# Another written order for SyncE's transfers and GpSimd's operations in a polysketch attention kernel with token mixing

## Chip, cores and metric

The kernel runs on one core of a Trainium2 chip. The metric is the device time of one execution in microseconds (us); the median of several runs is given. Engines are named as in the profile: PE (TensorE), DVE (VectorE), ACT (ScalarE), POOL (GpSimd) and SP (SyncE); SP and POOL are the two that issue DMA transfers here.

## The reference

Four batches, four heads, 1088 positions, head dimension 32, sketch size 8, so that all heads together are 128 wide. Inputs are float32, the weights arrive as float64.

```python
def phi(x):                                   # S1, S2: 8 x 32
    a = einsum('rd,bhsd->bhsr', S1, x)
    b = einsum('rd,bhsd->bhsr', S2, x)
    return einsum('bhsi,bhsj->bhsij', a, b).reshape(..., 64)
q_p, k_p = phi(q), phi(k)
kv = einsum('bhsf,bhsd->bhfd', k_p, v)
z = sum(k_p, axis=2)
x = einsum('bhsf,bhfd->bhsd', q_p, kv) / (einsum('bhsf,bhf->bhs', q_p, z) + 1e-6)
x = x.transpose(0, 2, 1, 3).reshape(4, 1088, 128)

theta = x @ w_theta
y = einsum('ts,bsd->btd', w_tok_r, x * cos(theta)) + einsum('ts,bsd->btd', w_tok_i, x * sin(theta))
u = x + y
out = u + maximum(u @ w_ch, 0)
```

The two token mixings, 1088 × 1088 × 128 for each of four batches and twice, are most of the arithmetic. They are computed with fewer products than that, in the manner of Strassen.

## The kernel before

**Tiles.** The 1088 positions are padded to nine chunks of 128. q, k and v of a batch are one tile of 128 partitions × 1152 columns each, in buffers of the class `big` (22 of 1152 columns). The token weights are 17 rows of blocks, each 1088 wide in two halves of 544; two half rows are loaded together as 64-bit words into a `zs` buffer (L614, 1088 KB) and rebuilt to float32: ACT makes a high part (L619) and a step (L621), DVE shifts the high part, and the step is added either by DVE or by an accumulating DMA that POOL issues (`join`, L348).

**The order is written out.** The program first records every operation (about 1150) with its engine, buffers and dependences; a call of `op` names the engine by a letter, "P" for PE, "V" for DVE, "A" for ACT, "G" for POOL, "S" for SP. Then `run` takes them in the order of the list `SEQUENCE`, whose numbers are the operations' indices, and gives each buffer the slot that the list `PLACES` says; `issue` emits them in that order. Each engine executes its own operations in the order of the list and waits for what they depend on, the former users of a slot included. No scheduler works after that.

**Stages, in order.** (1) `small`, `scaled`: the sketch matrices are unpacked, scaled and cut into parts. `rests` (L481) makes the sums `sf` and `sq`, `blocks_k` (L523) the head table `sbk` for the keys, `blocks_t` (L527) the table `sbt`, `sliced` (L491) the parts `cm`, `c16` and `cf`, `blocks_m` (L537) the head tables `mv` and `mf` of batch 0 for the queries, and `blocks_again` (L551) copies these to batches 1 to 3. `spread2` and `spread3` (L568, L589) serve a small product (L576) and its table `pbd`. All of these run on POOL.
(2) `key_sums` (L667): each batch's keys are rounded to a coarse level `kb` (bfloat16); PE sums kb·kb and the rest's products, from which a bound on the denominators is taken. For batches 1 to 3 the rest's product needs k + kb, which is made by loading k a second time into a buffer `kh` (L699, on SP) and adding kb to it with a `join` on POOL (stage names `keys1` to `keys3`; batch b's `rest` products on PE wait for it).
(3) `kfeatures`, `chain`, `query_slices`, `levels`: key features and their sums with v, and the queries' levels. `levels` (L1018) multiplies the queries by `mv` and `mf`; it is the first reader of the head tables.
(4) `numerators`, `theta_stage`, then the products of the mixing. Names in the prediction: `m70`, `m60`, `m30` are products of batches 0 and 1 (`product`, L1286) with sums of weight blocks; `ac30`, `ac20`, `ac40` (`asum`, L1275) are the accumulates that make these sums, eight `join`s each, one for each row block; `ac10` is such a sum on DVE. a11, a12, a21 and a22 are the quarters of the weights. `carry` adds a kept partial product to x by a `join`. `aj..` are the sums of smaller blocks later (L1525).

**Names of transfers.** `rowp3L` is the load and the rebuilding of the left halves of weight rows in pair 3, `rowp3R` the right halves, `row16` the last row. The lists below give POOL's and SP's share of the order.

```python
    def join(n, dst, src, w, r):                                                  # L346
        op("G", n * 2.55e-3, lambda: G.dma_start(dst(), src(), accum_op=ALU.add), w, r, kind=2)
    ...
        if KDMA[b]:                                                               # L697, batches 1 to 3
            op("S", n * 512 / 410e3, lambda: SY.dma_start(flat(kh()), k[b]...), [kh], [], kind=1)
    ...
        if KDMA[b]:                                                               # L707
            join(n, lambda: flat(kh()), lambda: flat(kb()), [kh], [kb])
    ...
    def run(self, sequence, places, fills):
        self.order = [self.ops[i] for i in sequence]
        for b, i in zip(self.bufs, places):
            b.slot = i
```

Of the kernel before, what the change touches and what calls it, by code (L numbers as in the profile page):

```python
# [52 lines left out]
    57, 58, 36, 233, 79, 10, 15, 54, 34, 59, 60, 61, 62, 95, 63, 51, 65, 66, 35, 38, 236, 131, 134, 16, 238,  # L53
    295, 136, 17, 67, 27, 182, 185, 68, 18, 69, 22, 137, 187, 241, 37, 183, 322, 242, 96, 237, 70, 239, 71, 72,
    73, 21, 210, 211, 212, 169, 306, 159, 74, 75, 80, 291, 293, 220, 296, 186, 28, 170, 29, 175, 221, 101, 243,
    81, 82, 83, 184, 346, 89, 176, 177, 297, 308, 30, 234, 244, 323, 240, 235, 84, 85, 86, 178, 222, 188, 213,
    90, 309, 307, 43, 87, 310, 326, 223, 102, 245, 163, 88, 311, 164, 91, 312, 214, 103, 19, 23, 246, 247, 248,
    92, 189, 215, 324, 386, 112, 104, 325, 93, 97, 44, 132, 105, 313, 347, 98, 463, 113, 39, 389, 455, 328, 464,
    249, 465, 466, 459, 460, 461, 462, 456, 457, 458, 171, 190, 191, 192, 193, 160, 99, 388, 194, 195, 196, 197,
    198, 133, 467, 33, 165, 20, 329, 261, 94, 166, 300, 108, 468, 114, 387, 172, 161, 469, 226, 135, 327, 139,  # L60
    470, 25, 350, 410, 348, 349, 471, 351, 100, 106, 199, 200, 162, 352, 298, 115, 107, 110, 472, 250, 201, 202,
    203, 204, 205, 353, 227, 206, 251, 252, 253, 262, 473, 207, 138, 394, 392, 109, 413, 299, 411, 474, 263,
    301, 140, 402, 475, 302, 208, 412, 254, 111, 255, 256, 257, 476, 258, 259, 264, 141, 142, 303, 46, 209, 260,
    45, 143, 144, 216, 145, 146, 477, 478, 147, 148, 149, 150, 151, 152, 267, 395, 397, 153, 268, 154, 390, 304,
    330, 155, 47, 24, 479, 403, 156, 157, 480, 481, 338, 484, 487, 485, 405, 491, 158, 269, 404, 265, 494, 492,
    173, 270, 266, 495, 482, 26, 271, 40, 305, 124, 483, 500, 493, 486, 48, 499, 332, 496, 391, 125, 488, 489,
    501, 272, 273, 497, 167, 490, 179, 118, 331, 274, 314, 502, 275, 116, 276, 126, 119, 277, 41, 120, 168, 174,
    503, 504, 505, 315, 450, 42, 341, 224, 180, 692, 632, 339, 127, 128, 217, 688, 689, 690, 506, 121, 340, 279,
    396, 684, 691, 218, 400, 693, 694, 122, 695, 685, 686, 687, 696, 283, 697, 498, 318, 278, 319, 117, 123,
    228, 698, 333, 699, 316, 515, 517, 282, 370, 700, 398, 229, 701, 702, 507, 509, 317, 181, 510, 452, 373,  # L70
    129, 511, 703, 230, 704, 219, 518, 354, 401, 508, 512, 130, 434, 516, 225, 526, 513, 231, 399, 524, 232,
    705, 286, 706, 709, 720, 710, 519, 451, 707, 708, 713, 525, 284, 520, 336, 521, 561, 514, 562, 563, 564,
    337, 371, 453, 557, 558, 553, 554, 555, 556, 408, 559, 716, 560, 334, 393, 436, 714, 723, 721, 362, 724,
    454, 634, 285, 715, 522, 717, 372, 335, 528, 565, 722, 711, 712, 342, 435, 566, 718, 344, 343, 356, 567,
    719, 355, 365, 725, 527, 726, 418, 409, 523, 568, 406, 569, 345, 570, 571, 730, 530, 732, 280, 281, 357,
    407, 635, 572, 531, 426, 529, 532, 533, 662, 727, 288, 748, 573, 574, 589, 542, 582, 750, 590, 591, 733,
    592, 593, 320, 585, 586, 583, 584, 419, 637, 594, 595, 587, 588, 575, 576, 321, 751, 578, 734, 608, 579,
    440, 736, 813, 577, 610, 821, 822, 823, 752, 374, 728, 739, 824, 747, 580, 364, 741, 375, 289, 376, 537,
    639, 377, 754, 742, 617, 729, 814, 437, 358, 441, 815, 416, 438, 611, 735, 749, 359, 816, 753, 817, 731,
    539, 612, 818, 439, 417, 819, 534, 743, 738, 740, 737, 755, 756, 414, 764, 758, 422, 745, 744, 619, 746,  # L80
    761, 763, 360, 361, 363, 757, 614, 415, 759, 420, 424, 378, 581, 820, 599, 368, 825, 826, 827, 613, 596,
    421, 762, 601, 620, 638, 621, 760, 536, 597, 598, 425, 607, 765, 609, 766, 772, 636, 369, 602, 603, 769,
    828, 366, 367, 538, 615, 600, 423, 605, 427, 627, 630, 829, 830, 831, 633, 616, 604, 606, 643, 428, 771,
    381, 379, 382, 774, 541, 430, 380, 626, 384, 629, 623, 645, 642, 429, 618, 432, 385, 640, 622, 383, 535,
    832, 442, 883, 768, 433, 624, 628, 540, 287, 833, 631, 834, 835, 836, 444, 448, 443, 446, 839, 840, 770,
    647, 641, 650, 658, 773, 644, 543, 655, 788, 837, 838, 544, 431, 767, 775, 777, 661, 646, 445, 653, 786,
    625, 841, 842, 844, 843, 845, 846, 667, 651, 670, 447, 776, 859, 449, 861, 927, 934, 648, 847, 660, 793,
    850, 778, 656, 649, 668, 791, 545, 652, 672, 789, 852, 657, 862, 863, 864, 669, 790, 1007, 865, 848, 867,
    659, 792, 665, 853, 679, 858, 654, 666, 928, 549, 779, 550, 860, 671, 866, 810, 849, 851, 546, 854, 855,
    794, 681, 683, 796, 663, 802, 801, 1009, 664, 856, 857, 877, 787, 868, 1025, 674, 798, 809, 800, 880, 1028,  # L90
    1026, 676, 870, 1010, 680, 682, 878, 871, 884, 881, 907, 1008, 890, 900, 872, 873, 806, 888, 547, 936, 892,
    909, 1014, 926, 678, 797, 869, 1032, 874, 902, 886, 1006, 891, 876, 932, 889, 875, 879, 548, 882, 911, 1027,
    804, 805, 893, 782, 1011, 887, 799, 894, 783, 551, 552, 807, 795, 1016, 1017, 895, 784, 803, 785, 906, 780,
    1029, 1046, 1012, 1018, 1019, 673, 1013, 1024, 1023, 898, 808, 1047, 1035, 1015, 904, 885, 899, 897, 896,
    912, 1044, 905, 677, 919, 910, 913, 916, 675, 903, 1031, 1022, 1020, 951, 811, 1030, 1045, 901, 940, 943,
    917, 933, 925, 915, 1021, 914, 918, 922, 1048, 1058, 1050, 812, 1053, 1049, 920, 924, 1060, 1033, 1037,
    1052, 923, 1051, 930, 945, 908, 929, 1034, 969, 1040, 931, 1041, 1054, 1056, 935, 1059, 1038, 937, 939,
    1057, 1062, 1055, 1061, 1070, 1071, 938, 946, 944, 947, 968, 1042, 1043, 1066, 1091, 1092, 1093, 962, 1039,
    781, 941, 942, 1065, 1064, 960, 1063, 1067, 1094, 950, 963, 1095, 1105, 952, 1096, 1097, 1098, 1068, 1069,
    1036, 1072, 1099, 1083, 961, 964, 1075, 1100, 1073, 1101, 1074, 1079, 1084, 1085, 949, 1076, 1080, 1081,  # L100
    948, 1102, 966, 1111, 958, 1077, 1078, 956, 965, 1086, 1082, 971, 957, 974, 973, 921, 967, 970, 972, 1087,
    975, 1088, 953, 982, 977, 983, 1110, 1089, 1090, 1002, 1003, 978, 979, 954, 959, 980, 976, 1004, 1005, 1106,
    981, 1123, 1112, 994, 995, 1116, 1104, 996, 987, 1109, 997, 1107, 990, 991, 1103, 992, 993, 1108, 984, 988,
    1130, 1133, 1134, 1115, 985, 955, 1125, 1135, 986, 989, 1114, 1117, 1121, 1126, 998, 1124, 999, 1000, 1136,
    1128, 1001, 1113, 1120, 1119, 1118, 1131, 1129, 1122, 1127, 1132, 1137, 1138, 1139, 1140, 1142, 1143, 1144,
    1145, 1141, 1146,
)
PLACES = (
    55, 59, 47, 48, 58, 2, 0, 2, 6, 7, 4, 11, 8, 21, 12, 7, 9, 24, 2, 46, 28, 3, 62, 61, 41, 45, 1, 60, 54, 47,
    56, 45, 46, 59, 48, 61, 51, 47, 54, 45, 61, 61, 41, 55, 49, 34, 60, 39, 58, 46, 36, 57, 44, 57, 52, 35, 54,  # L110
    47, 61, 49, 61, 56, 41, 60, 48, 36, 56, 42, 56, 50, 35, 55, 41, 61, 47, 34, 52, 50, 30, 9, 7, 60, 59, 43,
    53, 14, 59, 60, 16, 58, 43, 55, 38, 60, 40, 56, 34, 60, 43, 60, 37, 46, 51, 31, 10, 15, 59, 57, 39, 52, 13,
    57, 56, 60, 42, 58, 37, 56, 42, 60, 38, 55, 44, 62, 34, 29, 49, 29, 5, 12, 56, 62, 40, 45, 8, 55, 51, 47,
    52, 46, 53, 54, 59, 50, 45, 59, 46, 55, 51, 52, 53, 54, 49, 59, 50, 45, 61, 54, 53, 61, 40, 56, 58, 57, 32,
    56, 58, 56, 28, 55, 58, 56, 33, 57, 55, 58, 31, 17, 20, 18, 10, 3, 11, 1, 2, 13, 21, 14, 16, 8, 9, 6, 15,
    12, 22, 19, 23, 13, 26, 6, 23, 4, 22, 6, 24, 21, 26, 7, 24, 19, 25, 0, 22, 4, 25, 15, 26, 19, 26, 7, 22, 7,
# [1586 lines left out]
```

## Time and profile before

| what | value |
|---|---|
| runs | 222.5, 223.35, 222.51 us; median 222.51 |
| the profiled execution | 222.03 us |
| its span, first to last instruction | 220.3 us |
| PE clock granted | 1.00 |

How to read it. The span is the profiled execution from its first to its last instruction. A group or a waits row names line, engine and operation, and its tiles as out<-in; `[0.45 <-POOL sbk L334]` means that the engine stood idle 0.45 us before the instruction and that POOL's work on `sbk` ended that wait. In a timeline the first number is the start in us from the span's start, the second the duration. A `DMA_DIRECT2D` on POOL or SP is the issuing of a transfer; "DMA to landing" is the time from issue until the data is there. A table of stretches gives, for each, the busy time of PE, its weight loads, DVE, ACT and POOL with the count of instructions, the clock, the DMA engines' share and what they moved.

### The profile page before, as it was taken

Reading aid. Unit: us, or ns where it says so; the run is one execution under the profiler, and the core shown is the slowest. Engines: PE = TensorE matmul, PEld = TensorE weight load, DVE = VectorE, ACT = ScalarE, POOL = GpSimd, SP = SyncE. Lnnn points to the kernel's source line nnn. Section 1 sums busy time; section 2 is a strip of 40 time slices with the busy share of each in tenths; the row PEclk is TensorE's granted clock in tenths of the full one; section 3 lists DMA queues with packets and bytes.
Section 4 is the critical chain, followed back from the end, with each engine's and each line's share of the span. In section 5 each row is a group of like instructions: output and inputs, shape, how many; then the busy total and the mean of one; then the engine's idle time right before and its main releaser. Section 6 shows DMA issues by size and latency. Waiting matters only on the chain.

```text
span 220.3 us, 4200 instructions
## 1 busy us (share of the span) xinstructions
PE 212.1 (96%) x1481; PEld 177.1 (80%) x1481; DVE 188.1 (85%) x449; ACT 131.1 (60%) x277; POOL 80.7 (37%) x119
## 2 busy tenths in 40 slices
PE   7998999989999999999999999999999999999992
PEld 4697999976898796778888887888887888887882
DVE  2798999989999999999999999989999669567352
ACT  3896999979989899999989632662510100000000
POOL 1057934211013042064360746934360459251000
PEclk9999999999999999999999999999999999999999
DMA  6999999999759979987999999999998639688332
GB/s 207 407 415 409 349 354 389 358 419 376 233 171 285 296 239 226 316 210 124 190 261 176 276 192 189 189 183 189 185 134 124 96 46 149 93 122 112 61 56 53
DMA packets 34969, 48.78 MB, mean 221 GB/s; under 512 B 19204, under 2 KB 22276, under 8 KB 34820
## 3 DMA queue, kind: packets, MB, share of 16 engines
q0 software_dynamic: 10368, 18.21, 47.3%
q1 hardware_dynamic: 24580, 30.30, 40.8%
q8 instruction: 12, 0.20, 0.3%
q14 instruction: 9, 0.07, 0.1%
HBM read 28.07 MB, written 2.23 MB: 138 GB/s over the span
## 4 chain that ended last, share of the span: by engine, by line
PE 69%; DVE 18%; DMA 7%; issue 2%; ACT 2%; SPq 1%; ACTq 0%; DVEq 0%
PE ps L354 64%; DMA big<-hf 4%; DVE big L334 4%; DMA big<-k_l 3%; DVE g L334 3%; DVE big L338 2%; PE ps L1137 2%; DVE sm L341 2%; PE ps L1085 2%; DVE lv L334 1%; DVE sm L334 1%; DVE big L341 1%; ACT big L683 1%; DVE hf L338 1%; DVE zs L334 1%
## 5 line engine op out<-in xcount | busy, mean ns | idle before, releaser
L354 PE MATMUL ps<-big,zs 128*128 128x288 f32 (+3 forms) x450 | 107.3, 386 | 0.0
L354 PEld LDWEIGHTS ps<-big,zs 128*128 128x128 f32 x450 | 81.2, 190 | 18.4 <-DVE big L341 1.1
L348 POOL DMA_DIRECT2D big<-big x49 | 49.1, 1396 | 72.1 <-DVE big L338 24.0
L619 ACT ACTIVATE big<-zs 128x544 f32<-128x544 f32 x32 | 22.7, 721 | 1.8 <-DMA zs<-w_tok 1.8
L341 DVE SCALAR_TENSOR_TENSOR big<-ps,even,big 128x272 f32<-128x272 f32 (+3 forms) x34 | 16.1, 488 | 7.9 <-PE ps L354 7.8
L621 ACT ACTIVATE big<-zs 128x1088 int32<-128x1088 uint32 x16 | 19.6, 1225 | 0.7 <-DMA big<-big 0.5
L348 POOL DMA_DIRECT2D big<-hf x9 | 11.8, 1459 | 13.4 <-DVE big L334 6.9
L348 POOL DMA_DIRECT2D big<-g x10 | 9.8, 1112 | 18.4 <-DVE big L341 7.4
L1560 ACT ACTIVATE g<-ps,even 128x272 f32<-128x272 f32 x3 | 1.5, 488 | 22.4 <-PE ps L354 22.4
L354 PE MATMUL ps<-mf,big 128*128 128x96 f32 x72 | 14.4, 295 | 0.0
L338 DVE TENSOR_SCALAR big<-big 128x544 int32<-128x544 int32 (+1 forms) x33 | 14.0, 446 | 0.0
L1328 ACT COPY g<-ps 128x128 f32<-128x128 f32 x2 | 0.5, 266 | 21.8 <-PE ps L1326 21.8
L334 DVE TENSOR_TENSOR zs<-ps,g 128x768 f32<-128x768 f32 (+2 forms) x20 | 12.4, 630 | 1.0 <-issue 0.4
L354 PEld LDWEIGHTS <-hf 128*128 128x128 f16 (+1 forms) x144 | 12.2, 108 | 1.0 <-DVE hf L338 0.6
L341 DVE SCALAR_TENSOR_TENSOR big<-ps,big 128x288 f32<-128x288 f32 (+1 forms) x15 | 6.6, 438 | 7.4 <-PE ps L354 7.4
L354 PE MATMUL ps<-big,big 128*128 128x128 f32 x72 | 10.7, 280 | 1.1 <-DMA big<-hf 1.1
L334 DVE CUSTOM_DVE_ANT_0 big<-big,big 128x1088 uint16<-128x1088 uint16 x16 | 11.6, 729 | 0.1
L334 DVE TENSOR_TENSOR g<-lv 128x768 f32<-128x768 f32 x12 | 11.2, 954 | 0.3 <-PE ps L1137 0.2
L334 DVE TENSOR_TENSOR big<-big,hf 128x1152 f32<-128x1152 f32 x8 | 11.0, 1372 | 0.0
L354 PEld LDWEIGHTS ps<-mf,big 128*128 128x128 f32 x72 | 10.9, 191 | 0.0
L354 PE MATMUL ps<-w,big 128*128 128x128 f32 x76 | 10.5, 276 | 0.0
L354 PE MATMUL ps<-mv,hf 128*128 128x96 f16 x108 | 10.5, 206 | 0.0
(215 smaller groups left out, 442.6 us busy)
## 6 DMA issues: line engine op xcount, KB each, us to landing
zs<-w_tok SPq DMA_DIRECT2D x17, 1088.0 KB, 9.6
big<-big POOLq DMA_DIRECT2D x40, 272.0 KB, 7.3
big<-k_l SPq DMA_DIRECT2D x7, 576.0 KB, 6.6
big<-q_l SPq DMA_DIRECT2D x4, 576.0 KB, 8.8
big<-v_l SPq DMA_DIRECT2D x4, 576.0 KB, 11.3
big<-hf POOLq DMA_DIRECT2D x3, 576.0 KB, 9.3
big<-hf POOLq DMA_DIRECT2D x6, 272.0 KB, 6.4
big<-g POOLq DMA_DIRECT2D x10, 136.0 KB, 3.1
```

Of the source, the lines that this page charges most:

```text
L334: eng.tensor_tensor(out=o, in0=a, in1=b, op=f)
L338: (eng or V).tensor_scalar(out=o, in0=a, scalar1=s1, scalar2=s2, op0=op0, **kw)
L341: (eng or V).scalar_tensor_tensor(out=o, in0=a, scalar=s, in1=b, op0=op0, op1=op1)
L348: op("G", n * 2.55e-3, lambda: G.dma_start(dst(), src(), accum_op=ALU.add), w, r, kind=2)
L354: T.matmul(o, lhs, rhs, start=start, stop=stop, skip_group_check=True)
L619: op("A", 0.19 + HT * 0.0009, lambda j=j: A.activation(dst[j](), words()[1][:, j * HT:(j + 1) * HT].bitcast(F32), AF.Prelu, scale=scale, a ...
L621: op("A", 0.22 + S * 0.0009, lambda: A.activation(stp().rearrange("p r n -> p (r n)"), words()[0].bitcast(U32), AF.Copy, scale=2.0**-29), ...
L683: op("A", act(n) + 0.1, lambda: A.activation(flat(r()), kc(), AF.Square, accum_out=km()[:, 1:2]), [r, (km, 1)], [kx])
L1085: T.transpose(x()[:, i], xs()[:, off + i * P:off + (i + 1) * P], ident())
L1137: T.transpose(tr()[:, i * P:(i + 1) * P], qp()[:, i * H + 2 * n:i * H + 2 * n + 2].rearrange("p h i j -> p (h i j)"), ident())
L1328: op("A", act(P), lambda: A.copy(ot()[:, :P], tp()), [ot], [tp])
L1560: op("A", act(QT), lambda: A.mul(w(), to.out(0), evens[b]()[:, 5:6]) if b else A.copy(w(), to.out(0)), [w], [to.parts[0]] + ([evens[b]] if ...
```

## The change

Only the lists `SEQUENCE` and `PLACES` differ; every operation is there in both and does the same. PE's 421 operations, DVE's 343 and ACT's 248 come in the same order as before. Of POOL's 84 operations 69 stand at another place, of SP's 51 there are 16; 88 buffers have another slot (44 of them `big`). Two short pieces of the diff:

```diff
-    57, 58, 36, 233, 79, 10, 15, 54, 34, 59, 60, 61, 62, 95, 63, 51, 65, 66, 35, 38, 236, 131, 134, 16, 238,
-    295, 136, 17, 67, 27, 182, 185, 68, 18, 69, 22, 137, 187, 241, 37, 183, 322, 242, 96, 237, 70, 239, 71, 72,
+    57, 58, 36, 233, 79, 10, 21, 15, 54, 34, 59, 60, 61, 62, 95, 63, 51, 65, 35, 66, 236, 131, 134, 38, 37, 16,
+    238, 295, 136, 17, 67, 182, 185, 68, 186, 69, 137, 187, 241, 183, 242, 96, 70, 20, 239, 71, 72, 73, 210,
...
-    850, 778, 656, 649, 668, 791, 545, 652, 672, 789, 852, 657, 862, 863, 864, 669, 790, 1007, 865, 848, 867,
-    659, 792, 665, 853, 679, 858, 654, 666, 928, 549, 779, 550, 860, 671, 866, 810, 849, 851, 546, 854, 855,
-    794, 681, 683, 796, 663, 802, 801, 1009, 664, 856, 857, 877, 787, 868, 1025, 674, 798, 809, 800, 880, 1028,
+    927, 934, 648, 847, 793, 850, 778, 649, 668, 791, 545, 652, 672, 789, 852, 862, 863, 864, 794, 657, 669,
+    790, 1007, 865, 848, 867, 659, 792, 665, 853, 679, 858, 654, 666, 928, 801, 549, 779, 550, 860, 671, 866,
+    810, 849, 851, 546, 854, 855, 681, 683, 802, 1009, 856, 857, 877, 787, 868, 1025, 800, 663, 674, 809, 880,
```

In names, POOL's first operations:

- before: `spread2`, `rests`, `blocks_t`, `blocks_k`, `spread3`, `keys3`, `sliced`, `blocks_m`, `keys2`, `tiny`, `blocks_again` (batch 2), `keys1`, `blocks_again` (1, 3), `rowp0R`, one `ac30`, …
- after: `blocks_k`, `tiny`, `rests`, `spread2`, `blocks_t`, `spread3`, `sliced`, `keys2`, `keys3`, `blocks_m`, `blocks_again` (3, 2), `keys1`, `blocks_again` (1), `rowp1R`, …

SP's first loads:

- before: q0, small, k0, k3, k1, k2, q2, q1, rowp0L, kh3, kh2, rowp3L, w2, rowp0R, q3, v0, kh1, rowp3R, rowp1R, rowp2R, rowp1L, rowp2L, v1, v2, row16, v3, …
- after: q0, small, k0, k3, k1, k2, q2, q1, kh2, w2, rowp0L, kh3, rowp3L, kh1, rowp0R, q3, v0, rowp3R, rowp1R, rowp2R, rowp1L, v3, v1, v2, rowp2L, row16, …

POOL's accumulates between about 94 and 110 us of the profile before (numbers are indices of operations):

- before: `ac30` 635, `carry0_1`, `ac30` 637, 639, `rowp6R` 441, 439, `rowp3R` 417, 415, `ac30` 638
- after: `rowp2R` 407, 409, `ac30` 637, 632, 635, 636, 639, `rowp3R` 417, `rowp6R` 441, 439, `carry0_1`, `rowp3R` 415

and from about 123 us on:

- before: `rowp5R` 433, `ac20` 658, 655, `rowp5R` 431, `ac20` 653, `rowp7R` 447, 449, `ac20` 660, 656, 657, 659, 654, `ac40` 794, 796, `carry1_0`, `ac40` 801, `carry1_1`, `ac40` 798, 800, 797, `carry3_0`, `carry3_1`, `ac40` 799, 795, `aj51` 1017, 1019, 1013, 1015
- after: `rowp5R` 431, `ac20` 655, `rowp5R` 433, `ac20` 658, 653, 656, `rowp7R` 447, 449, `ac20` 660, `ac40` 794, `ac20` 657, 659, 654, `ac40` 801, 800, `carry1_0`, `carry1_1`, `ac40` 798, 797, 796, `carry3_0`, `carry2_1`, `ac40` 799, `aj51` 1015, 1017, `ac40` 795, `aj51` 1013, 1019

Among the last stores, out2_0_1 and out2_0_0 go ahead of out0_0_0 and out0_0_1, which was the other way round.

128 rows, old and new, of tables (PLACES, SEQUENCE) are left out of this document.

## The prediction, made before the changed kernel was run

> **What bounds the kernel now.** I read the page first (share of each engine, chain), then TensorE's list of waits, then the timelines around those waits, and last the transfers' landings.
>
> ```profile
> span 220.3 us, 4200 instructions
> PE 212.1 (96%) x1481; PEld 177.1 (80%) x1481; DVE 188.1 (85%) x449; ACT 131.1 (60%) x277; POOL 80.7 (37%) x119
> ...
> PE 69%; DVE 18%; DMA 7%; issue 2%; ACT 2%; SPq 1%; ACTq 0%; DVEq 0%
> ...
> PE ps L354 <- DMA big<-hf: 1.1, 1, 1.1
> PE ps L354 <- POOL sbk L334: 0.4, 1, 0.4
> PE ps L354 <- DVE sm L883: 0.3, 1, 0.3
> PE ps L354 <- ACT sm L842: 0.3, 1, 0.3
> ```
>
> TensorE works 212.1 of 220.3 us and its order is not changed. So the question is only which of its waits go and which come; the waits column is total, count, longest. The largest inside the kernel is 1.1 us on one transfer; after 57.3 us TensorE runs on almost without a gap, so whatever makes it late stays.
>
> ```profile
> 19.70 0.60 PE L354 MATMUL ps<-sbt,sm 128*128 128x64 f32 x4 [0.45 <-POOL sbk L334]
> 21.97 0.83 PE L354 MATMUL ps<-sm,pbd 128*128 128x64 f32 x6 [0.17 <-ACT sm L866]
> ...
> 27.42 0.43 PE L354 MATMUL ps<-mf,big 128*128 128x96 f32 x2
> ...
> 36.72 0.71 PE L354 MATMUL ps<-big,big 128*128 128x128 f32 x4
> 37.71 2.40 PE L354 MATMUL ps<-big,big 128*128 128x128 f32 x20
> ...
> 45.67 2.27 PE L354 MATMUL ps<-big,big 128*128 128x128 f32 x18 [1.06 <-DMA big<-hf]
> ```
>
> The columns are start, duration, engine, line, what. 36.72 begins the second batch's key-rest products, 37.71 the third's follow among them, 45.67 the first's: it waits 1.06 us for the accumulate of batch 1's keys (L348).
>
> **Part 1, the key transfers earlier: −1.06.** That accumulate could not be issued before its target, the second copy of k (L699), was there, and SyncE asked for it late:
>
> ```profile
> 24.67 0.33 SPq L699 DMA_DIRECT2D big<-k_l  x1
> big<-k_l SPq DMA_DIRECT2D x7, 576.0 KB, 6.6
> 36.25 0.91 POOL L348 DMA_DIRECT2D big<-hf  x1 [6.85 <-DVE big L334]
> DMA to landing us min/median/max: 9.4/9.4/9.4
> ```
>
> Issue at 36.25 plus 9.4 is 45.6, the matmul's start. After, SyncE asks for it ahead of q3 and v0, some 11 us sooner; GpSimd then issues the accumulate behind the third set of head tables: by part 2 at 28.75 and two copies of the tables, at most as long as the 1.70 there, 32.2. With the same 9.4 us it lands at 41.6, 3 us before the matmul could start (45.67 − 1.06 = 44.61). The wait goes: −1.06. Bounds −1.06 and 0.
>
> **Part 2, the head tables behind two key accumulates: +1.3.** These are GpSimd's operations before:
>
> ```profile
> 20.33 0.85 POOL L334 TENSOR_TENSOR pbd<-psc,hm 128x128 f32<-128x128 f32 x2 [1.02 <-DVE psc L338]
> 21.13 1.03 POOL L348 DMA_DIRECT2D big<-hf  x1
> 21.93 1.25 POOL L338 TENSOR_SCALAR cm<-sc 128x8 f32<-128x8 f32 x1
> 23.39 1.20 POOL L495 CAST c<-cm 128x16 f16<-128x16 f32 x1
> ...
> 25.19 0.23 POOL L338 TENSOR_SCALAR cf<-sf 128x8 f32<-128x8 f32 x1
> ...
> 25.53 0.44 POOL L334 TENSOR_TENSOR mv<-s,hm 128x32 f16<-128x32 f32 x2
> ...
> 26.75 0.48 POOL L334 TENSOR_TENSOR mf<-cf,hm 128x32 f32<-128x32 f32 x2
> 27.17 0.91 POOL L348 DMA_DIRECT2D big<-hf  x1
> ```
>
> The tables (L540 through L541) are ready at 27.23, and the first matmul that needs the last of them starts at 27.42: nothing to spare. Before, one accumulate (21.13, next operation 0.80 later) stood ahead of them and the second (27.17) behind; after, both stand between `sliced` and the tables. `sliced` itself can start at 21.15, once `pbd` is done, but not run through it:
>
> ```profile
> 21.73 1.35 DVE L334 TENSOR_TENSOR big<-big,hf 128x1152 f32<-128x1152 f32 x1
> 23.17 1.37 DVE L334 TENSOR_TENSOR big<-big,hf 128x1152 f32<-128x1152 f32 x1
> 27.20 0.75 DVE L338 TENSOR_SCALAR hf<-big 128x1152 f16<-128x1152 f32 x1
> ```
>
> An eight-column operation on GpSimd takes 1.25 us (21.93) while VectorE's 1152-column one runs and 0.23 us (25.19) outside; both long ones end when VectorE's does. VectorE's order stays. After, the first three operations of `sliced` fit in from 21.15 on, the fourth is held to VectorE's end at 23.08, the fifth to 24.54, and the last two (0.23 each) end it near 25.1. Two accumulates at 0.80: 26.7. Tables 25.53 to 27.23, 1.70: 28.4. One of them meets VectorE's 0.75 at 27.20; half of it, 0.35: 28.75, against 27.42 that is +1.3. Bounds: accumulates that cost 0.4 each and no such meeting, 25.1 + 0.8 + 1.7 = 27.6, +0.2; 1.03 and 0.91 each, full 0.75: 29.5, +2.1. I take the middle, which is nearest to the 0.80 row. This also means that the gain of part 1 isn't on its own: with tables 1.3 late the old wait at 45.67 would have been swallowed; together the two parts make +0.24.
>
> [...]
>
> **Part 3, `rests` ahead of `spread2`, `blocks_k` and `tiny` first: 0.** The small product of line 577 comes later by the moved operations, some 0.65 us; it is needed for the 19.70 and 21.97 matmuls, whose own waits of 0.45 and 0.17 (rows above, 0.62 together) take it up. If not: +0.6.
>
> **Part 4, the weight accumulates of the late stretch one place later: +0.8.** From 125 to 159 us the transfers are the tight resource:
>
> ```profile
> 136.00:140.00 4.00, 4.00 (x62) 3.07 (x35) 3.96 (x11) 1.60 (x5) 3.76 (x7) 1.00 1.10 193
> 140.00:144.00 4.00, 4.00 (x21) 3.32 (x21) 3.83 (x12) 3.97 (x9) 4.00 (x5) 1.00 1.10 185
> ...
> L348 POOL DMA_DIRECT2D big<-big x2: 862/1037/1212, 136.2 to 136.8; - x2
> DMA to landing us min/median/max: 6.7/7.1/7.5
> ...
> 142.63 3.35 PE L354 MATMUL ps<-big,zs 128*128 128x256 f32 x14
> 145.81 0.59 PE L354 MATMUL ps<-big,w 128*128 128x256 f32 x2
> 146.45 0.42 DVE L341 SCALAR_TENSOR_TENSOR big<-ps,big 128x256 f32<-128x256 f32 x1 [0.80 <-PE ps L354]
> ```
>
> The last two columns of the stretches are the DMA share (over 1: full) and GB/s. One such accumulate is 128 × 544 × 4 bytes, 278.5 KB, and at 190 GB/s takes 278.5/190 = 1.47 us; the two issued at 136.24 and 136.78 land at 142.9 and 144.25, 1.35 apart: a place in this queue is worth about 1.45 us. The last of them, the sum for a21's row block 1 (ac20), feeds m60's last block: four of the fourteen matmuls that end where 145.81 begins, (145.81 − 142.63)/14 × 4 = 0.91, so 144.90. After, ac40's block 0 goes ahead of the last three ac20 sums: the last lands at 144.25 + 1.45 = 145.70, 0.80 after the need. Bounds: 0.3, if the lateness of parts 1, 2 and 5 (0.6) comes on TensorE alone while the queue keeps its times; 1.4, if VectorE is also held by the two sums before it (late by 0.3 and 0.9, of which its 0.80 wait at 146.45 hides most). I take 0.8, the row's own figure: this queue is fed by ScalarE and VectorE, which follow TensorE.
>
> **Part 5, other moves: +0.4.** In the stretch before, an accumulate for row pair 6 now stands behind row pair 3's and one more sum:
>
> ```profile
> 102.32 2.64 POOL L348 DMA_DIRECT2D big<-big  x3 [4.55 <-ACT big L621]
> DMA to landing us min/median/max: 3.4/3.9/4.4
> 108.95 1.17 ACT L1191 ACTIVATE big<-big 128x1152 f32<-128x1152 f32 x1
> ...
> 158.37 0.41 ACT L1533 ACTIVATE big<-lv 128x272 f32<-128x272 f32 x1
> 166.25 0.62 PE L354 MATMUL ps<-big,hf 128*128 128x272 f32 x2
> ```
>
> The second of the three lands at 102.86 + 4.4 = 107.3, and in the new placement of buffers ScalarE's operation at 108.95 writes one that it reads; two places of 1.45 make it 110.2: 0 to 1.2 late, taken as 0.4, since ScalarE has slack against TensorE there. ac40's block 1 moves behind accumulates that follow ScalarE's copy at 158.37; m30's last block needs it just before 166.25. It is issued near 160; at 4.4 us it lands in time, at 7.1 about 1.5 late: taken as 0. rowp2L behind three loads of v, and the first output pair's order: 0, their readers come after the landing.
>
> **Sum** against the profiled execution's 222.03: −1.06 + 1.3 + 0 + 0.8 + 0.4 = +1.44, 223.47. The median of the runs, 222.51, stands 0.48 over the profiled one: 222.51 + 1.44 = 223.95.
>
> **The rivals.**
> - *The wait simply goes* (faster): the tables are covered after all, because GpSimd's operations slip between VectorE's, and the late queue has room. 222.51 − 1.06 = 221.45; with the small waits behind it (0.3 and 0.3) 220.85. For it: the wait's row is plain. Against it: 27.23 against 27.42 leaves no cover. It decides if the tables are ready by 27.5.
> - *Early parts cancel, the late places are hidden*: +0.24, 222.75. For it: the late stretch's queue may shift as a whole with ScalarE.
> - *The key accumulates crowd each other* (slower still): three of 576 KB took from 21.13 to 45.6, 24.5 us, with SyncE's transfers beside them. After, the first starts only at 25.1 and the next 0.8 later, so if 7 us each is what the queue grants, the second lands at 25.1 + 2 + 14 = 41 where 37.71 + 1.3 = 39.0 is needed, 2.0 later than part 2 allows for, and the key wait is back in another place: 222.51 + 1.3 + 2.0 − 1.06 + 1.2 = 225.95; halfway 225. Against it: k's second copies no longer compete with them. The point is whether the third batch's rest products (37.71) wait on a transfer.
>
> [...]
>
> **How the numbers follow.** Forecast 0.42 (223.95, from 223.2 to 224.8), wait simply gone 0.18, cancel 0.17, crowding or a late block 1 of ac40 0.23. About 0.5%, 1.1 us, is what a measurement can tell from no change: faster is under 221.4, slower over 223.6. Slower: 0.30 of the forecast's, 0.22 of the last, 0.01 elsewhere, together 0.53; faster: 0.14 of the first rival's; the rest is 0.33. The range goes from 221.4, where the first rival's lower half is left out, to 226.2, the crowding case with 0.25 over.
>
> **What would show it.** No wait of TensorE on a key accumulate at 45.67: part 1. A new wait of about 1.3 us before the first matmuls on `mv` and `mf`, on POOL: part 2. A wait of about 0.8 before m60's last block on a transfer: part 4. A wait at the third batch's rest products means crowding. The forecast is wrong if TensorE meets none of these, or if the head tables are ready by 27.5.

## The result, and the profile after

| | before | changed |
|---|---|---|
| median of 20 runs each, us | 222.31 (221.59 to 225.34) | 226.34 (222.97 to 231.53) |
| ratio, changed to before | | 1.0099, 95% interval 1.0071 to 1.0127 |
| the profiled execution, us | 222.03 | 226.04 |

The ratio puts the changed kernel 2.2 us (1.6 to 2.8) slower, at about 224.5; it leaves out ten of the changed kernel's 20 executions, which the 226.34 includes: eight with a low granted clock (at a mean of 0.965 to 0.981 they took 227.4 to 231.5 us) and two of 226.49 us. The prediction was 223.95. The profiled execution is 4.0 us slower, so it is one with more of the loss than the mean.

The page of the changed kernel, its head and the shares of the chain:

```profile
span 224.3 us, 4193 instructions
PE 212.5 (95%) x1481; PEld 177.0 (79%) x1481; DVE 188.2 (84%) x449; ACT 131.3 (59%) x277; POOL 82.0 (37%) x119
...
PE 42%; DMA 8%; issue 6%; POOL 2%; ACT 2%; DVE 0%; ACTq 0%; POOLq 0%
```

PE's busy time is 0.4 us over that of before (212.1); the other 3.6 us are idle time. Its timeline where it waits:

```profile
18.30 0.43 PE L354 MATMUL ps<-psc,sx 8*128 8x64 f32 x2 [0.39 <-POOL psc L572]
...
28.04 0.20 PE L354 MATMUL ps<-mv,hf 128*128 128x96 f16 x1 [0.70 <-POOL mv L334]
28.42 0.20 PE L354 MATMUL ps<-mv,hf 128*128 128x96 f16 x1 [0.18 <-POOL mv L334]
28.80 0.20 PE L354 MATMUL ps<-mv,hf 128*128 128x96 f16 x1 [0.18 <-DVE g L334]
29.18 0.46 PE L354 MATMUL ps<-mf,big 128*128 128x96 f32 x2 [0.18 <-POOL mf L334]
...
117.95 0.55 PE L1085 MATMUL ps<-ident,g 128*128 128x128 f32 x3 [2.49 <-ACT g L1077]
...
148.72 0.97 PE L354 MATMUL ps<-big,zs 128*128 128x288 f32 x3 [0.30 <-DMA big<-big]
```

The wait of 1.06 at 45.67 is gone. New are the waits for the head tables (four, 1.24 together), one of 2.49 at 117.95 and one of 0.30 at 148.72. Setting each matmul's start beside the same matmul's of before gives where PE falls behind: 0.05 ahead at 19.70 (of before), 1.77 behind at 27.42, 0.55 at 45.67 and still 0.55 at 92.5, 3.21 at 114.74, 3.36 at 142.63, 3.82 at 144.90, 3.93 at the end. So: tables +1.8, key wait −1.25, middle +2.66, m60 +0.6. POOL's early operations show the first of these:

```profile
24.86 0.18 POOL L499 COPY cf<-sf 128x8 f32<-128x8 f32 x1
24.99 1.98 POOL L348 DMA_DIRECT2D big<-hf  x2
26.36 1.62 POOL L334 TENSOR_TENSOR mv<-s,hm 128x32 f16<-128x32 f32 x2
...
28.16 0.97 POOL L334 TENSOR_TENSOR mf<-cf,hm 128x32 f32<-128x32 f32 x2
```

`sliced` ends at 25.04, then come the two key accumulates and only at 26.36 the tables (25.53 before), which are finished at 28.16 + 0.97 = 29.13 (27.23 before). The middle, POOL and ACT:

```profile
87.01 1.73 POOL L348 DMA_DIRECT2D big<-big  x2 [4.53 <-DVE big L338]
98.28 7.18 POOL L348 DMA_DIRECT2D big<-big  x8 [9.54 <-DVE even L341]
...
113.62 1.16 ACT L1191 ACTIVATE big<-big 128x1152 f32<-128x1152 f32 x1 [4.01 <-DMA big<-big]
```

POOL issues rowp2R's two accumulates (407, 409), then stands for 9.54 us, and then issues eight transfers one behind the other. ACT waits 4.01 us for the eighth, rowp6R's second, and PE's 2.49 at 117.95 follows from that. The row names DVE's small work on `even`, which ends at that moment; but the first of the eight, the sum 637, adds to the row block that 409 is filling. In the kernel before, 409 stood ahead of 407; issued at 81.0, it took 10.2 us and had landed at 91.2, before the first sum of this stretch was issued (94.16). POOL's semaphore wait and the landings of the two transfers before it and of three up to rowp6R's second (the last number is the longest) read:

```profile
L348 POOL DMA_DIRECT2D big<-big x2: 854/1026/1198, 87.0 to 87.5; - x2
L348 POOLq EVENT_SEMAPHORE  x1: 10367/10367/10367, 87.4 to 87.4; - x1
...
DMA to landing us min/median/max: 7.8/9.0/10.2
...
L348 POOL DMA_DIRECT2D big<-big x3: 1561/1710/2061, 102.1 to 103.4; - x3
...
DMA to landing us min/median/max: 7.6/8.4/10.1
```

409 landed at 87.55 + 10.2 = 97.8, POOL's wait lasted from 87.4 for 10.37 us, to 97.8 as well, and it goes on at 98.28; in e1 to e6 below, too, the sum 637 is issued 0.52 us after 409's landing. rowp6R at 103.41 + 10.1 = 113.5, against 107.3 before.

### The profile page after: what moved, and what is told of

It is laid out like the page before. It is cut to its first block, busy times and chain, and to the rows that moved or that the text cites. A ratio compares the mean times of both kernels' runs of the same rounds, so it can differ in the third digit from the quotient of the medians.

```text
span 224.3 us, 4193 instructions
## 1 busy us (share of the span) xinstructions
PE 212.5 (95%) x1481; PEld 177.0 (79%) x1481; DVE 188.2 (84%) x449; ACT 131.3 (59%) x277; POOL 82.0 (37%) x119
## 4 chain that ended last, share of the span: by engine, by line
PE 42%; DMA 8%; issue 6%; POOL 2%; ACT 2%; DVE 0%; ACTq 0%; POOLq 0%
PE ps L354 41%; DMA big<-big 8%; POOL big L348 2%; PE ps L1085 1%; ACT big L1191 1%; ACT g L1077 0%; ACT g L1094 0%; ACT g L1097 0%; DVE big L341 0%; PE ps L1326 0%; DVE g L341 0%; ACT g L1328 0%; ACTq L1191 0%; ACT big L621 0%; POOLq L348 0%
## 5 line engine op out<-in xcount | busy, mean ns | idle before, releaser
L348 POOL DMA_DIRECT2D big<-big x49 | 47.6, 1337 | 86.8 <-PE ps L1003 32.7
L348 POOL DMA_DIRECT2D big<-g x10 | 10.5, 1236 | 18.9 <-DVE big L341 10.4
L334 DVE TENSOR_TENSOR zs<-ps,g 128x768 f32<-128x768 f32 (+2 forms) x20 | 12.4, 630 | 0.7 <-issue 0.4
```

The source lines that it names most:

```text
L334: eng.tensor_tensor(out=o, in0=a, in1=b, op=f)
```

## Experiments

Each is the changed kernel with an edit of its lists, unless it says otherwise. "Net" is how far PE is behind the kernel before, less what it is behind at 19.70 already: the first loads land differently from execution to execution (k0 4.2 us after its issue before, 4.7 in the changed kernel), and PE was 0.05 ahead there in the changed kernel, 0.69 behind in e2. A later wait can take such lateness up, as e2 shows, so a net gain can be too large by as much.

### e1: the middle stretch

```diff
-  ac30 637, 632, 635, 636, 639, then rowp3R 417, rowp6R 441, 439
+  ac30 632, 636, 639, 635, 637, then rowp3R 417, rowp6R 441, 439
```

> The changed kernel with one edit: the five ac30 sums of the stretch at 94 to 110 us go in the order 632, 636, 639, 635, 637 instead of 637, 632, 635, 636, 639; rowp3R and rowp6R stay behind all five. Theory A (POOL stands at 637 until the accumulate of row block 5, issued last before it, has landed at 97.76, and the whole queue behind starts 4 us late): POOL issues three sums by 90 us, rowp6R's second accumulate lands near 109.5 instead of 113.51, ScalarE's L1191 waits under 1 us instead of 4.01, TensorE's wait of 2.49 at 117.95 is gone, and the profiled span is 221.5 to 222 instead of 224.3. Theory B (part 5 of the prediction as it was put: two more places of 1.45 us in a full queue, whatever opens it): the number of accumulates ahead of rowp6R is the same, so it lands within 1 us of 113.5 and the wait of TensorE stays over 1.5 us.

POOL's timeline and the landing of rowp6R's two:

```profile
87.33 4.39 POOL L348 DMA_DIRECT2D big<-big  x5 [4.17 <-DVE big L338]
93.58 0.90 POOL L348 DMA_DIRECT2D big<-big  x1 [1.85 <-DMA big<-big]
95.30 0.86 POOL L348 DMA_DIRECT2D big<-big  x1 [0.82 <-DVE g L334]
102.46 2.63 POOL L348 DMA_DIRECT2D big<-big  x3 [6.31 <-DVE big L338]
...
DMA to landing us min/median/max: 5.0/5.5/5.9
```

Theory A. Three sums are issued at once behind rowp2R, rowp6R lands at 103.73 + 5.9 = 109.6 with the same accumulates ahead of it, ACT doesn't wait for it, PE's 2.49 is gone, and the span is 221.4. rowp6R is issued no sooner than in the changed kernel (103.41 there); what is gone is the backlog ahead of it. Theory B, my own step, falls. The profiled execution took 223.92 us; the other three took 226.98, 230.55 and 230.56 us at a mean clock of 0.969 to 0.983, so the trace shows the wait gone, but the times alone show no gain.

### e2: the same blocking order in the kernel before

```diff
-  rowp2R 409, 407, ac30 635, carry0_1, 637, 639
+  rowp2R 407, 409, ac30 637, 635, carry0_1, 639
```

> The kernel before with one edit: rowp2R's accumulates 407 and 409 swapped, and the ac30 sum 637, which needs 409's landing, put first among the sums (637, 635, carry0_1, 639 instead of 635, carry0_1, 637, 639). Nothing else of the change is in it, and as many accumulates stand ahead of rowp6R as before. Theory A (a sum at the head that waits for a late landing holds the queue): POOL's sums start at 97 to 98 us instead of 94.16, rowp6R lands 2 to 3 us later than its 107.3, 109.5 to 110.5, ScalarE's L1191 starts 0.5 to 1.5 us late; TensorE waits 0 to 1 us near 115; time +0 to +1 us. Theory B (places in the queue alone): no place is changed, rowp6R at 107.3 within 0.5, time the same within 0.3.

Ratio 1.0014 (0.9993 to 1.0036): no change that can be told.

```profile
86.63 1.75 POOL L348 DMA_DIRECT2D big<-big  x2 [4.17 <-DVE big L338]
95.53 1.75 POOL L348 DMA_DIRECT2D big<-big  x2 [7.16 <-issue]
...
103.73 2.63 POOL L348 DMA_DIRECT2D big<-big  x3 [4.47 <-ACT big L621]
```

POOL stands again until 409 has landed, but here that was at 95.0, and it had idle time left (4.47) before rowp6R. So the wait at the head costs nothing with a landing at 95.0 and three sums behind it; how much of that is the landing and how much the number of sums (five in the changed kernel) isn't shown. rowp6R's second landed at 108.7, between the two theories' ranges, so this run doesn't tell them apart. Its PE wait of 0.8 near 92 has another cause, ACT held for 2.12 us, up to 88.69, by the last weight row's accumulate.

The run shows one thing more, on part 1. Its early order is that of before, yet PE doesn't wait for batch 1's key accumulate:

```profile
35.15 0.90 POOL L348 DMA_DIRECT2D big<-hf  x1 [5.08 <-DVE sm L338]
DMA to landing us min/median/max: 9.5/9.5/9.5
...
45.31 2.23 PE L354 MATMUL ps<-big,big 128*128 128x128 f32 x18
```

It landed at 44.6, before PE came there, and PE is 0.36 ahead of the profile before at 45.67, although it was 0.69 behind at 19.70 (net 1.05), with nothing changed up to there. So the wait of 1.06 is not in every execution of the old early order.

### e3: the head tables first

```diff
-  sliced, keys2, keys3, blocks_m, blocks_again 26, 25, keys1
+  sliced, blocks_m, keys2, keys3, blocks_again 26, 25, keys1
```

> The changed kernel with one edit: blocks_m ahead of the key accumulates of batches 2 and 3, as the order before had it ahead of the second of them. Part 2 as predicted: the tables are ready by 27.2 or sooner, TensorE's waits at 28.04 to 29.18 (1.24 in all) are gone, the first key accumulates start at 26.8 instead of 24.99 and land about 1.8 later, the third stays at 31 to 32 and lands by 44, in time, so TensorE at the first batch's rest products (46.22 in the changed kernel) is about 1.2 earlier, 45.0 or less; what follows at 117.95 depends on that stretch and may take it back. Rival (the accumulates crowd each other): the two key accumulates, later by 1.8, make the rest products of batches 2 and 3 wait by 0.5 to 2 us, and the gain at 46.22 is under 0.5.

Ratio 1.0123 (1.0066 to 1.018). The tables' waits are gone, but PE and the landing of the two accumulates, issued at 27.2 and 28.0, read:

```profile
41.13 1.05 PE L354 MATMUL ps<-big,big 128*128 128x128 f32 x7 [2.59 <-DMA big<-hf]
...
DMA to landing us min/median/max: 10.1/11.6/13.1
```

The rival's mechanism, and larger than it said: the second lands at 28.02 + 13.1 = 41.1, and PE waits 2.59 for it; net 1.7 at 45.67. A key accumulate issued by itself took 9.1 to 9.4 us from issue to landing in the kernel before, batch 1's 9.5 in e2 and 9.4 in e11; the second of a pair took 12.4 in the changed kernel and 13.1 here. The changed kernel has the crowding too, but there the pair is issued 2.2 us sooner, ahead of the tables, and lands at 38.2 without a wait of PE; that is what part 2's loss buys. The wait at 117.95 is absent here: 409 landed at 96.6, and PE comes there 1.7 us later than in the changed kernel.

### e4: ac40's block 0 back behind ac20

```diff
-  ac20 660, ac40 794, ac20 657, 659, 654
+  ac20 660, 657, 659, 654, ac40 794
```

> The changed kernel with one edit: ac40's block 0 behind the last ac20 sum, as before. Part 4 as predicted: the last ac20 sum lands a place, 1.3 to 1.5 us, earlier against the sum ahead of it, the wait of 0.30 at 148.72 and the shift of 0.6 us of TensorE there are gone, the end is 0.6 sooner with the 2.49 at 117.95 still there (span 223.7 if that wait is the same size). Rival (the wait is set by when POOL may issue, after TensorE has read the old block, not by the place): the shift there stays within 0.2 of 0.6.

Ratio 1.0128 (1.0083 to 1.0174). No wait at 148.7 is left, and from 142.63 of before on PE loses nothing instead of 0.56. The other profiles agree: with block 0 ahead of the last ac20 sums PE loses 0.35 there in e1, 0.19 in e5, 0.27 in e10 and nothing in e3; with it behind them, nothing in e6 to e9, e11 and e12. In its profile the wait of the middle was

```profile
117.06 0.55 PE L1085 MATMUL ps<-ident,g 128*128 128x128 f32 x3 [1.30 <-ACT g L1077]
```

1.30, not 2.49: 409 had landed 0.7 us sooner. The mechanism of part 4 is borne out; the ratio cannot show 0.5 us, since the middle's wait varies by more.

### e5 and e6: the early order as before, with the early key load; then everything mended

```diff
 e5
-  spread3, sliced, keys2, keys3, blocks_m, blocks_again 26, 25, keys1
+  spread3, keys3, sliced, blocks_m, keys2, blocks_again 26, 25, keys1
 e6: e5 with the edits of e1 and e4
```

> The changed kernel with the early part of POOL's order as before but for the first batch's key accumulate: keys3 ahead of sliced, blocks_m ahead of keys2 (keys2 then the copies of the tables and keys1, at about 31). Nothing late is changed. Part 1 alone as predicted: the tables are ready by 27.3, keys3 lands near 30.5, keys2 near 36.5, keys1 by 43, so no key wait is left at 36 to 46 and TensorE is 0.8 to 1.1 us ahead of the kernel before at the first batch's rest products (45.67 there), against 0.55 behind in the changed kernel. The late waits (2.49 at 117.95 or part of it, 0.3 at 148.7) stay or grow by as much as TensorE comes earlier. Rival (the accumulates crowd each other whatever their order, as in the run with the tables first): a wait of over 0.5 us on a key accumulate at 36 to 46 and a gain there under 0.5.

> The changed kernel with the early order of the run above, the ac30 sums in the order 632, 636, 639, 635, 637, and ac40's block 0 behind the last ac20 sum. If the three causes are all that there is, only part 1 is left: TensorE 0.8 to 1.1 us ahead of the kernel before all the way to the end, span near 219.3, time 221.0 to 221.6 against about 222.2, ratio 0.995 to 0.998. Rival (a further cause in the changed order or the placement of buffers): a wait of TensorE over 0.5 us that neither kernel had, time 222.2 or more.

e5: ratio 1.006 (1.0019 to 1.0101), PE net 0.05 ahead at 45.67 where 0.8 to 1.1 was expected; e6: 1.0156 (1.0109 to 1.0203), the rival. No key wait is left in either; PE waits for another transfer, first e5's row, then e6's:

```profile
34.43 0.44 PE L354 MATMUL ps<-g,big 128*64 128x128 f32 x4 [0.99 <-DMA big<-v_l]
```

```profile
35.70 0.55 PE L354 MATMUL ps<-g,big 128*64 128x128 f32 x6 [2.24 <-DMA big<-v_l]
```

v of batch 0, late, was hidden in the changed kernel behind the tables' delay: issued at 24.62, it made no wait, since PE comes to it only at 34.77 there. e6 shows a second thing, in its stretches from 34 us on (after the stretch and its length: busy time of PE, its weight loads, DVE, ACT, POOL; then the granted clock, the DMA share, GB/s):

```profile
34.00:36.00 2.00, 0.30 (x6) 0.33 (x8) 1.93 (x8) 2.00 (x6) 0.00 (x0) 1.00 1.04 329
36.00:38.00 2.00, 2.00 (x21) 1.83 (x18) 2.00 (x5) 0.34 (x1) 0.00 (x0) 0.78 1.07 329
38.00:40.00 2.00, 2.00 (x17) 1.70 (x17) 0.39 (x2) 1.28 (x3) 0.00 (x0) 0.50 1.01 391
40.00:42.00 2.00, 2.00 (x24) 1.83 (x21) 2.00 (x5) 0.96 (x5) 0.00 (x0) 0.87 1.02 420
```

Behind the wait the clock falls to half: the losses of 0.22, 0.50 and 0.13 over 2 us each are 1.7 us. PE is net 3.06 behind at 45.67: 2.7 by the wait and one of 0.19 ahead of it, 1.6 by the clock, less 1.25. The middle and the end add 0.1, so the edits of e1 and e4 hold. In e5 409 landed at 95.1, and its middle has no wait on rowp6R although its order is the changed one; it has one of 0.82 at 92.09 on ACT, of e2's cause.

### e7: the two late edits alone

```diff
 the edits of e1 and e4
```

> The changed kernel with the two late edits alone (ac30 sums in the order 632, 636, 639, 635, 637; ac40's block 0 behind the last ac20 sum), the tables behind the two key accumulates as in the changed kernel. Left are parts 1 and 2: TensorE 0.5 to 0.9 us behind the kernel before at the end, span 220.9 to 221.3, time 222.8 to 223.2. Rival: a further late cause, a wait of TensorE over 0.4 us after 90 us.

Ratio 1.0327 (1.0251 to 1.0403), far over both theories; three of the four executions had a mean clock of 0.958 to 0.969 and took 228.6 to 232.4 us, the profiled one took 225.13 at 0.99. The rival's wait is there, 0.65 at 93.85 on ACT, of e2's cause, but it costs under 0.6. Most of the loss is early, as the waits for the tables and the stretches behind them tell:

```profile
28.53 0.20 PE L354 MATMUL ps<-mv,hf 128*128 128x96 f16 x1 [0.71 <-POOL mv L334]
28.91 0.20 PE L354 MATMUL ps<-mv,hf 128*128 128x96 f16 x1 [0.18 <-POOL mv L334]
29.30 0.20 PE L354 MATMUL ps<-mv,hf 128*128 128x96 f16 x1 [0.18 <-DVE g L334]
29.68 0.35 PE L354 MATMUL ps<-mf,big 128*128 128x96 f32 x1 [0.18 <-POOL mf L334]
```

```profile
28.00:30.00 2.00, 0.93 (x6) 0.52 (x6) 2.00 (x3) 2.00 (x6) 2.00 (x11) 1.00 1.01 334
30.00:32.00 2.00, 2.00 (x24) 1.99 (x22) 2.00 (x4) 1.32 (x2) 2.00 (x6) 0.80 1.02 291
32.00:34.00 2.00, 2.00 (x16) 1.98 (x15) 0.96 (x3) 0.32 (x2) 1.57 (x5) 0.50 1.05 329
34.00:36.00 2.00, 2.00 (x22) 1.99 (x22) 0.42 (x2) 1.27 (x3) 0.00 (x0) 0.85 1.08 326
```

Again half the clock for a time that costs 1.7 us, here behind four waits of which none is longer than 0.71.

### e8: v in another buffer

```diff
 e6, and in PLACES
-  v0: slot 7, sx of the first den: slot 2
+  v0: slot 2, sx of the first den: slot 7
```

> The kernel of the run with all three mended, with one more edit: the first batch's v gets the buffer that k of batch 0 leaves at 20.7 (slot 2, as in the kernel before) instead of the one that k of batch 2 leaves at 24.5 (slot 7); the first den's buffer sx takes slot 7. Theory: the wait of 2.24 us on v0 at 35.7 there (0.99 in the run before it) came from this buffer, not from the order of transfers; with it gone no wait over 0.4 us is left in 20 to 46, the granted clock stays 1.00 throughout, TensorE is 0.5 to 1.0 ahead of the kernel before at 45.67 there, and the time is 221.2 to 221.9, ratio 0.995 to 0.999. Rival: v0 is late because the second k of batch 1 and two halves of weights are ahead of it on SyncE's queue; v0 then still lands after 33.5, a wait of 0.4 to 1.5 us on it remains, and the time is 222.2 or more.

Ratio 1.0013 (0.9983 to 1.0044). SyncE issues v0 at 21.31 instead of 24.71 and PE's row is

```profile
34.11 0.66 PE L354 MATMUL ps<-g,big 128*64 128x128 f32 x8 [0.50 <-DMA big<-v_l]
```

Both theories hold in part: the buffer cost part of v0's delay, and a wait remains with the transfers ahead of it. PE is net 0.3 ahead at 45.67 and at the end; if its 0.6 of lateness at 19.70 isn't taken off, it is 0.3 behind. In three of the twelve executions the mean clock was 0.981 to 0.985 (226.4 to 228.0 us).

### e9, e10, e12: PE kept busy at the tables

```diff
-FILLS = ((290, 1), (64, 14))
+FILLS = ((290, 1), (64, 14), (463, -8))     e9 on e7, e10 on the changed kernel
+FILLS = ((290, 1), (64, 14), (463, -3))     e12 on e7
```

An entry puts matmuls on idle data ahead of an operation, here the first levels product.

> The kernel with the two late edits alone (which ran at 225.1 us with a granted clock of 0.50 in 32 to 34 us, right behind the waits for the head tables) with one more edit: eight matmuls on idle data, about 1.3 us, ahead of the first batch's first levels product, so that TensorE isn't idle while it waits for the tables. Theory (the idle time at 28 to 30 us makes the clock halve for some 3 us, and this, not a wait, is what puts that kernel 2 us over its sum): clock 1.00 in 28 to 40 us, TensorE 0.5 to 1.0 behind the kernel before at 45.67 there instead of 2.67, time 222.8 to 223.4. Rival (the clock follows something else, such as the load of the whole chip): a clock under 0.95 in 28 to 40 us in the profile, or times of 225 and more as before.

> The changed kernel with the eight matmuls on idle data ahead of the first levels product and nothing else. Theory (idle time at the tables lowers the clock in some executions): mean clock of every run 0.985 or more, all runs between 222.9 and 226.3 (the waits at 117.95 and 148.7 are still there). Rival: runs with a mean clock of 0.975 or less and 229 us or more come as with the changed kernel itself, in about 8 of 20.

> The kernel with the two late edits and, ahead of the first levels product, three matmuls on idle data instead of eight (each took 0.38 us, so eight made TensorE 1.9 us later than the tables did; three take 1.1, what the waits for the tables take). Theory: clock 1.00 in 28 to 40 us, TensorE 0.5 to 0.9 behind the kernel before at 45.67 there as counted from 19.70 on, and at the end 0.5 to 1.1 behind, time 222.8 to 223.5. Rival: the clock falls to 0.5 there in some executions (mean under 0.98), or a late wait of over 0.4 us brings the end to 1.5 and more behind.

e9 with its eight:

```profile
27.85 2.97 PE L388 MATMUL ps<-idle 128*128 128x384 bf16 x8
```

```profile
28.00:30.00 2.00, 1.72 (x6) 0.48 (x5) 2.00 (x3) 2.00 (x6) 2.00 (x10) 1.00 1.03 348
30.00:32.00 2.00, 1.83 (x18) 1.22 (x17) 2.00 (x3) 0.94 (x1) 2.00 (x6) 1.00 1.01 297
32.00:34.00 2.00, 2.00 (x28) 2.00 (x28) 1.12 (x3) 0.67 (x2) 1.73 (x5) 1.00 1.07 332
```

The clock stays at 1.00, and the mean clock was 0.995 or more in all 16 executions of the three kernels. They ran on other chips than e7, so the chip is not excluded as a cause; on that of e9 and e10 the kernel of e8 had its three low ones. e10 kept to its expected times, e9 and e12 did not: the eight took 2.97 us, over twice what I had put, and made PE 3.0 late at the tables (net), 1.2 more than the tables do. They start 0.38 us apart, such matmuls at 6.6 to 8.9 us of the profile before 0.16 apart; what makes the difference isn't shown. Ratios 1.0133 (1.0074 to 1.0191) for e9, 1.0112 (1.0064 to 1.016) for e10, 1.0056 (1.0021 to 1.0091) for e12. In e12 PE is net 0.8 behind at 45.67, as expected, but 2.0 at the end: its profiled execution has a wait of 0.83 at 93.40 on ACT, of e2's cause.

### e11: v0 ahead of the early key load

```diff
 e8, and on SyncE
-  rowp3L, kh1, rowp0R, q3, v0
+  rowp3L, rowp0R, q3, v0, kh1
```

> The kernel of the run with v in slot 2, with one more edit on SyncE: the second load of batch 1's keys (kh1) goes behind v0 instead of ahead of rowp0R, q3 and v0. SyncE asks for it at about 21.1 (24.67 in the kernel before, 11.4 in the changed one). Theory (0 to 45 us is bound by the transfers; each one put ahead makes another late, and v0 is needed first, at 33, the key accumulate only at 44.6): v0 lands by 32.9, no wait on it; kh1 lands by 34.5, its accumulate is issued by then and lands by 43.9; no wait over 0.4 in 20 to 57 other than those of 51 and 57; TensorE 0.7 to 1.0 ahead of the kernel before at 45.67 there as counted from 19.70 on; time 221.2 to 221.9, ratio 0.995 to 0.999. Rival: the accumulate, issued later, lands after 44.6 again (9.4 us from 35.5 on), a wait of 0.3 to 1.0 is back, and the time is the same as before within 0.2 per cent.

Ratio 1.001 (0.9987 to 1.0033). The head of the list of PE's waits (total, count, longest):

```profile
PE ps L388 <- POOL idle L390: 1.3, 1, 1.3
PE ps L354 <- DVE sm L883: 0.6, 1, 0.6
PE ps L354 <- POOL psc L572: 0.6, 1, 0.6
PE ps L1137 <- ACT g L725: 0.3, 1, 0.3
...
```

No wait on a transfer is left, and PE is net 1.25 ahead at 45.67 (e2, with the old early order: net 1.05). It keeps 0.64 of the net: the wait at 47.7 (ACT, 0.27) is new and that at 57.0 (DVE) is 0.65 instead of 0.33. In its profile 0.42 of lateness at 19.70 takes most of the rest, and the times show no gain: 222.64 against 222.74 of the kernel before, run beside it. None of the versions beats the kernel before.

## Why the prediction was right, and where it was not

- **Part 1 (−1.06).** The wait went, as said: 1.25 net in the profiled execution. But e2 has no such wait with the old early order either, so the prediction took for a fixed cost what varies, and how much is gained on the mean isn't shown. What made the wait go, the load ahead of q3 and v0, together with v0's new buffer made v0 late (waits of 0.99, 2.24 and 0.50 on it in e5, e6 and e8), which the tables' delay hid in the changed kernel; the prediction put v0's place at nothing. And PE kept only about 0.6 of it in e11.
- **Part 2 (+1.3).** Right in mechanism and nearly in size: +1.8 at 27.42, 1.24 of it waits in four pieces, the rest because the first product's matmuls, released one by one (28.04, 28.42, 28.80), no longer follow each other closely: 0.38 apart, where before the three took 0.29 together from 27.25 on. `sliced` ended at 25.04 (25.1 predicted), the two accumulates took 1.3 us (1.6 predicted) and the tables 2.8 (2.05 predicted), so the sum is nearer than its terms. e3 shows what the prediction had only as a rival: the tables cannot go first without the key accumulates coming 2.6 late. Parts 1 and 2 together: +0.6, predicted +0.24.
- **Part 3 (0).** Right: a wait of 0.39 at 18.30, and at 19.70 PE is where it was; the 0.45 there took it up.
- **Part 4 (+0.8).** Right in mechanism (e4): 0.56 in the profiled execution, 0.30 of it seen as a wait, 0 to 0.35 in the others with that order.
- **Part 5 (+0.4).** The step that failed, in reason and size. I counted two more places in the queue for rowp6R, 0 to 1.2 us late at ACT. It came 4.0 late, because the sum at the head waits for 409's landing while POOL, which issues in order, holds the seven transfers behind it (POOL idle for 9.54 us; e1: same places, another head, no wait). 409 landed between 95.1 and 97.8 in the executions with this order profiled here (e3, e4 and e5 among them), and PE's wait was 2.49, 1.30 or none. With e1's edit ACT waits for rowp6R in none of e6 to e9, e11 and e12, where 409 lands at 94.9 to 97.5. In e10, with the changed order and 409 at 97.5, PE itself comes 1.8 us later and has no wait, so its own lateness counts too. I infer from this, without traces of the other executions, that it is most of the spread of the changed kernel's compared times (222.97 to 226.18).
- **Not in the prediction:** the clock. It halved right behind the waits for the tables in e7 and behind another wait in e6; with PE kept busy at the tables no such fall is in the three profiles from 20 to 48 us, and the mean was 0.995 or more in all 16 executions (e9, e10, e12). A mean of 0.97 over 229 us is an estimated 6.9 us of lost clock, about four falls such as e7's of 1.7; no execution with so low a mean was profiled, so where they lie isn't shown. Why it falls in some executions and not in others stays open.

The sum of the terms, 1.44, was under the measured 2.2, inside its range: part 1 and 2's +0.24 was +0.6, and part 5's +0.4 lies between 0 and 2.66 from execution to execution. That the total came so near is in part luck: part 5's reason was wrong, and the median of all 20 executions, 226.34 with the low clocks in it, is just over the top of the range.

## What to carry to other kernels

On an engine that issues in order, rank operations by when their own inputs land, not only by when their results are needed: one early need with a late input held eight transfers for 9.5 us here. Where the transfers are full (a DMA share of 1.00 to 1.07 from 20 to 48 us of the changed kernel), a load put ahead takes its time from another (a wait of 0.50 on v0 with batch 1's keys ahead of it in e8, none with v0 ahead in e11); look for the next reader whose slack is smallest before counting a wait as gained, and for a late reader that something else hides at present. A gap in an otherwise full TensorE may cost more than its length (1.7 us of clock behind 2.24 us of waits in e6 and behind 1.25 in e7).

## What the runs showed of the hardware that I had not expected

In e6 and e7 the granted clock fell to 0.50 for an estimated 3.4 us, if in one piece (37.1 to 40.5 and 31.2 to 34.6; from the slices, 0.85 × 2 / 0.5), some 1.5 us after the waits had ended: in e6 a single wait of 2.24 us, in e7 four waits of 1.25 us in all. In e3 a wait of 2.59 left it at 1.00, and so did the 2.49 in the changed kernel. The length of a wait alone doesn't decide it, then: in e7 none of the waits right ahead of the fall was longer than 0.71 us. What does, these runs don't show.
